# Clustered attention with two MLPs: the first head's first stacks written by copies, the third pair's norms two slots later, the first row of minima issued by ScalarE

## The chip, the cores and the metric

The kernel runs on one core of a Trainium2 chip. The metric is the device time of one execution in microseconds (us). The engines are named as in the profile: PE (TensorE, with PEld for its weight loads), DVE (VectorE), ACT (ScalarE), POOL (GpSimd) and SP (SyncE, which only issues transfers).

## The reference

The inputs are q, k and v (2 batches, 8 heads, 768 positions, 64 columns), 16 centroids a head, and the weights of two MLPs. Attention runs only between positions whose query and key have the same nearest centroid:

```python
q_n = q / (norm(q) + 1e-06)          # k_n, c_n in the same way
q_assign = argmax(einsum('bhsd,hcd->bhsc', q_n, c_n), axis=-1)
k_assign = argmax(einsum('bhsd,hcd->bhsc', k_n, c_n), axis=-1)
scores = q @ k.T / sqrt(64)
scores = where(q_assign[..., None] == k_assign[..., None, :], scores, -1e9)
scores = scores - max(scores, axis=-1)
attn = exp(scores); attn = attn / (sum(attn, axis=-1) + 1e-09)
x = (attn @ v), all heads side by side          # 1536 x 512
x = ((x @ w1) * (x @ w2)) @ w3 @ w_out          # first MLP
out = softplus(x @ w_in) @ w_out2               # second MLP
```

## The kernel before

**Pairs and slots.** The 16 heads are handled in 8 pairs; head hd is 2*pi + j. A head has 6 chunks of 128 queries, and the attention loop has one slot for each (96, and 10 more to drain). In slot s, `mx_pe` multiplies one chunk of queries with all keys into the PSUM bank mb (two matmuls, L600), and `mx_red` takes the extreme value of each row from it (L609, tile mn, a TENSOR_REDUCE on VectorE). There is one such bank, so the matmuls of a slot wait for the reduction of the slot before. Every 6 slots `m_row` turns a head's six columns of minima into a row (L616, L63, tile mr) and a DMA (L620) puts it into the head's q tile. Nine slots after its minima a chunk's scores are computed (`st_pe`, L630), exponentiated (`st_exp`, L637), and one slot later multiplied with v (`av_pe`, L645).

**Stacks.** The matmuls do masking and splitting in one go, by stacking rows: a head's tiles q and k have 128 rows and two parts, n = 0 and 1. Rows 0 to 63 hold the high part H of the transposed q or k, rows 64 to 95 a piece of the other operand's low part L, rows 96 and on the one-hot of the cluster (part 0), or the row of minima and a row of ones (part 1). The minima need part 0 alone. H and L come from a transpose (`t1_pe`, L307) and its evictions (`t1_ev`, L318 on ScalarE, L319 on VectorE); both hold q in rows 0 to 63 and k in rows 64 to 127, one tile for each head of a pair. `t_dma` moves them into the stacks by seven DMAs (L335 to L340), issued by SP, after a memset of the row of ones (L333, POOL). The one-hot rows go from PSUM to a tile sg (`back_ev`, L416) and from there by DMA (`m_dma`, L422).

**The clusters of a pair.** `load_qk` (L198) loads q and k of a pair into rawqk, of which there is one buffer. `norm_sq` squares it (L256 on POOL, or L258 on ScalarE), `norm_fold` adds pieces on POOL (L266, from the third pair on), `norm_sum` adds up on VectorE (L274), then come the root and reciprocal (L281 to L297). `sims_pe` and `simsT_pe` multiply with the centroids (L353, L373), `assign` finds the best cluster (L386 to L400), `back_pe` transposes the one-hots back (L410).

**The centroids** are normalised at the start on VectorE, in column operations (`centroid_prep`, L215 to L228).

**What sets the order.** Everything runs in the order in which it is written, under a manual schedule: each engine takes its instructions in that order and waits for what they need. The first pair is handled ahead of the slots. The second pair's steps are listed by slot in the tables PE1 and EV1, those of the later pairs in PE and EV, as an offset from the pair's first slot 2*QC*pi (QC is 6), so that the entry -18 of the third pair falls in slot 6. `steps` goes through these. Beside all this runs the preparation of the weight product (`w_step`, lines L63 and L465 to L474: load, scale, bits; w3r and w3d are its tiles). Its first two tiles are decoded between the first pair's one-hots and the first slot's minimum.

Of the kernel before, what the change touches and what calls it, by code (L numbers as in the profile page):

```python
# [9 lines left out]
F32R = mybir.dt.float32r  # L10
BF16 = mybir.dt.bfloat16
I32 = mybir.dt.int32
AF = mybir.ActivationFunctionType
# [5 lines left out]
P = 128  # L19
# [3 lines left out]
def f32(ap):  # L23
    return ap.bitcast(F32)
# [3 lines left out]
def fused_kernel(ctx: ExitStack, tc, q, k, v, centroids, w1, w2, w3, wo, w_in, w_o2, out):  # L28
# [6 lines left out]
    nc = tc.nc  # L35
    B, H, S, D = q.shape
# [153 lines left out]
    def load_qk(pi, js=range(2), dma=dma_in):  # L190
        if pi >= NPAIR:
            return
        b, h0 = divmod(2 * pi, H)
        if js[0] == 0:
            QK[pi] = ap1.tile([P, 2, QC, 2, D], F32, tag="rawqk", name=f"rawqk{pi}")
        for j in js:
            for ni, src in enumerate((q, k)):
                dma(  # L198
                    QK[pi][:, j, :, ni, :], src[b, h0 + j].rearrange("(p c) d -> p c d", p=P)
                )  # L200
# [51 lines left out]

    def norm_sq(pi, j):
        sq = ring.tile([P, QC, 2, D], F32, tag="w3k", name=f"sq{pi}_{j}")
        if pi >= 2:
            nc.gpsimd.tensor_tensor(out=sq, in0=QK[pi][:, j], in1=QK[pi][:, j], op=ALU.mult)  # L256
        else:
            nc.scalar.activation(sq, QK[pi][:, j], AF.Square)  # L258
        PR["sq", j] = sq
# [65 lines left out]
    def t_dma(pi, j):  # L325

        hd = 2 * pi + j
        a, l = f32(PR["H", j]), f32(PR["L", j])  # L330
        qt = QT[hd] = apT.tile([P, 2, S], F32R, tag="q", name=f"q{hd}")
        kt = KT[hd] = apT.tile([P, 2, S], F32R, tag="k", name=f"k{hd}")
        nc.gpsimd.memset(f32(kt[96:97, 1, :]), 1.0)  # L333
        dma = nc.sync.dma_start
        dma(f32(qt[:D]), a[:D].unsqueeze(1).to_broadcast([D, 2, S]))  # L335
        dma(f32(kt[:D, 0, :]), a[D:])
        dma(f32(kt[:D, 1, :]), l[D:])
        for n in range(2):
            dma(f32(qt[D : D + 32, n, :]), l[32 * n : 32 * n + 32])
            dma(f32(kt[D : D + 32, n, :]), a[D + 32 * n : D + 32 * n + 32])  # L340

    SG = ((0, 512), (512, S))

    def sims_pe(pi, g):
        if g == 0:
            PR["sT"] = ring.tile([P, S], F32, tag="w3k", name=f"sT{pi}")
        h0 = (2 * pi) % H
        m = take()
        c0, c1 = SG[g]
        n = 0  # L350
        for j in range(2):
            for t in (PR["H", j], PR["L", j]):
                nc.tensor.matmul(  # L353
                    m[:, : c1 - c0], cst[:, h0 + j, :], t[:, c0:c1],
                    start=(n == 0), stop=(n == 3),
                )
                n += 1
        PR["sm", g] = m
# [53 lines left out]

    def back_ev(pi):

        sg = PR["sg"] = ring.tile([P, S], F32R, tag="w3k", name=f"sg{pi}")
        nc.scalar.activation(sg, PR["bk"][:, :S], AF.Copy, scale=bigcol[:, 0:1])  # L416
        give(PR["bm"])
# [195 lines left out]
    def m_row(g):  # L613

        m = take()
        nc.tensor.transpose(m[:QC, :P], MN.pop(g), identF)  # L616
        t = sp.tile([QC, P], F32R, tag="mr", name=f"mr{g}")
        act_copy(t, m[:QC, :P], scale=-1.0)
        give(m)
        nc.sync.dma_start(f32(QT[g][96:97, 1, :]), f32(t))  # L620


    def st_pe(j):
# [200 lines left out]
    def pgo(o, f, *a):  # L824
        tc.cur_priority -= o
        f(*a)
        tc.cur_priority += o

    def steps(tab, s):
        for pi in range(2, NPAIR):  # L830
            for f, *a in tab.get(s - 2 * QC * pi, ()):
                if f is not load_qk or pi > 2:
                    f(pi, *a)


    PE1 = {
# [2 lines left out]
    }  # L839
    EV1 = {  # L840
        0: [(t1_ev, 0), (norm_sq, 0)], 1: [(t1_ev, 1), (norm_sum, 0)], 2: [(t1_ev, 2), (norm_sq, 1), (t_dma, 0)],
        3: [(t1_ev, 3), (norm_sum, 1), (norm_root,)], 4: [(sims_ev, 0), (norm_rec, 0), (norm_rec, 1), (t_dma, 1)],
        5: [(sims_ev, 1), (norm_rec, 2)], 7: [(assign, 0)], 8: [(assign, 1)],
        9: [(back_ev,)], 10: [(m_dma, 0), (m_dma, 1)],
    }

# [9 lines left out]
    with tc.manual_schedule():  # L856
        act_dma = nc.scalar.dma_start
        load_qk(0, [0])
        centroid_load()
        load_qk(0, [1], act_dma)  # L860
        nc.scalar.preload_act_table_set("natural_log_exp_and_others")
        w_load()
        w_load()
        t1_pe(0, 0)
        t1_pe(0, 1)
        centroid_prep()
        t1_ev(0, 0)
        t1_ev(0, 1)
        t1_pe(0, 2)
        t1_pe(0, 3)  # L870
        t1_ev(0, 2)
        t1_ev(0, 3)
        t_dma(0, 0)
        centroid_turn()
        norm_sq(0, 0)
        norm_sq(0, 1)
        sims_pe(0, 0)
        sims_pe(0, 1)
        sims_ev(0, 0)
        sims_ev(0, 1)  # L880
        norm_sum(0, 0)
        norm_sum(0, 1)
        simsT_pe(0)
        norm_root(0)
        norm_rec(0, 0)
        norm_rec(0, 1)
        norm_rec(0, 2)
        t_dma(0, 1)
        load_qk(1)
        assign(0, 0)  # L890
        assign(0, 1)
        back_pe(0)
        back_ev(0)
        m_dma(0, 0, act_dma)
        m_dma(0, 1, act_dma)
        w_load()
        load_v(0)
        while wk[0] < W0:
            w_next()
        for s in range(NSLOT + ML + AL):  # L900
            j = s - ML
            a = j - AL
            if s < NSLOT:
                mx_pe(s)
                mx_red(s)
            if s and s % QC == 0 and s <= NSLOT:
                m_row(s // QC - 1)
            weights = s >= ML
            if weights:
                w_step(wk[0], "hlpqe")  # L910
            if a > 0 and a % 3 == 0:
                av_ev(a // 3 - 1)
            for tab in (PE1, EV1):
                for f, *x in tab.get(s, ()):
                    f(1, *x)
            if s == 4:
                load_qk(2)
            if s == 6:
                load_v(1)
            steps(PE, s)  # L920
            steps(EV, s)
            if 0 <= j < NSLOT:
                st_pe(j)
                st_exp(j)
            if weights:
                w_step(wk[0], "Abcds")
            if 0 <= a:
                av_pe(a)
            if weights:
                w_step(wk[0], "Tm")  # L930
                wk[0] += 1

            for g in range(NH):
                r = s - (ML + AL + QC * g + QC - 1)
                if r in (2, 4, 6):
                    r_ev(g, r // 2 - 1)
                if r == 8:
                    x_norm(2 * g)
                    x_norm(2 * g + 1)
            if wk[0] == NWSTEP:  # L940
                feed.load(3)
            if s == NSLOT + 1:
                feed.take(2)
                taken += 2
# [176 lines left out]
```

## Time and profile before

| | |
|---|---|
| Time, median of 3 runs | 859.72 us (858.72 to 859.75) |
| Profiled execution | 858.86 us, span 857.1 us |
| Busy share of the span | PE 94%, DVE 58%, ACT 46%, POOL 28% |
| First matmuls of the minima (slot 0) | 28.00 us after the span's start |

The profile shows one execution; its span runs from the first instruction to the last, and the time of the execution is 1.76 us longer. The shares are means over the whole program; the attention loop and the MLPs behind it keep PE nearly full, its beginning does not.

### The profile page before, as it was taken

The page shows a single profiled execution, that of the slowest core. Times are in us where ns is not written, and L with a number is a line of the kernel's source. Part 1 is how long each engine was busy: PE and PEld are TensorE (multiplying, and loading weights), DVE is VectorE, ACT ScalarE, POOL GpSimd, SP SyncE. Part 2 cuts the span into 40 slices and gives each one's busy share as a digit, 9 for nine tenths or more (in the row PEclk, how much of TensorE's full clock was granted, in tenths as well). Part 3 has the DMA queues.
Part 4 walks back from the last instruction along what each step waited for, and adds up shares of the span by engine and source line. Part 5 has one row for each costly group of instructions (what it writes and reads, how often), then busy time and mean ns, then how long its engine had stood idle before and what let it go on. Part 6 is the DMA issues. An engine that isn't in the chain of part 4 may idle for free.

```text
span 857.1 us, 10095 instructions
## 1 busy us (share of the span) xinstructions
PE 801.5 (94%) x3553; PEld 636.8 (74%) x3553; DVE 492.9 (58%) x823; ACT 396.5 (46%) x683; POOL 242.7 (28%) x229
## 2 busy tenths in 40 slices
PE   4549999998999999989999999999999999999997
PEld 3337677776777777758888888887877788888886
DVE  5646766575676564438453254663988644454442
ACT  3315454454453444464443235454564644455443
POOL 2032333153414021135411113231344222222221
PEclk9969999999999999999999999999999999999999
DMA  7755756646545354026511114340120000001001
GB/s 195 186 106 136 182 133 137 162 115 171 154 111 119 85 157 104 21 68 185 169 49 50 50 50 147 99 148 0 50 74 1 25 26 1 1 0 50 1 1 50
DMA packets 77827, 76.40 MB, mean 89 GB/s; under 512 B 46416, under 2 KB 62928, under 8 KB 77776
## 3 DMA queue, kind: packets, MB, share of 16 engines
q1 hardware_dynamic: 76016, 74.96, 33.0%
q10 hardware_dynamic: 1760, 0.79, 0.4%
q8 instruction: 28, 0.46, 0.2%
q14 instruction: 23, 0.19, 0.1%
HBM read 50.41 MB, written 3.24 MB: 63 GB/s over the span
## 4 chain that ended last, share of the span: by engine, by line
PE 73%; DVE 12%; DMA 6%; issue 3%; ACT 2%; SPq 2%; POOL 1%; ACTq 0%; DVEq 0%; POOLq 0%
PE avb L645 10%; PE rb L793 8%; PE sb L793 8%; PE sb L1009 6%; PE mb L1052 6%; PE sb L630 6%; PE rb L1009 5%; PE rb L515 5%; PE mb L815 4%; PE mb L600 3%; PE rb L1052 3%; PE avb L1052 3%; PE avb L815 2%; PE rb L815 2%; DVE mn L609 2%
## 5 line engine op out<-in xcount | busy, mean ns | idle before, releaser
L609 DVE TENSOR_REDUCE mn<-mb 128x1 f32<-128x768 f32 x96 | 91.6, 954 | 92.5 <-PE mb L600 92.2
L645 PE MATMUL avb<-E,v 128*128 128x384 f32 x384 | 142.4, 493 | 0.4 <-ACT t L61 0.4
L66 POOL TENSOR_TENSOR u<-u,t 128x512 f32<-128x512 f32 x48 | 68.4, 1427 | 170.5 <-DVE u L1032 170.5
L637 ACT ACTIVATE E<-sb 128x768 f32<-128x768 f32 x96 | 77.7, 809 | 68.0 <-PE sb L630 67.0
L630 PE MATMUL sb<-q,k 128*128 128x384 f32 (+1 forms) x384 | 91.3, 360 | 7.6 <-ACT E L637 7.6
L645 PEld LDWEIGHTS avb<-E,v 128*128 128x128 f32 x384 | 71.9, 192 | 28.3 <-ACT t L61 1.8
L600 PE MATMUL mb<-k,q 128*128 128x384 f32 x192 | 69.8, 446 | 20.2 <-DVE mn L609 15.6
L630 PEld LDWEIGHTS sb<-q,k 128*128 128x128 f32 (+1 forms) x384 | 66.9, 193 | 14.1 <-ACT E L637 11.2
L1009 PE MATMUL sb<-ys,wh_i 128*128 128x512 f32 x192 | 64.1, 395 | 3.5 <-ACT t L1020 2.3
L600 PEld LDWEIGHTS mb<-k,q 128*128 128x128 f32 x192 | 36.0, 202 | 41.0 <-DVE mn L609 21.4
L1009 PE MATMUL rb<-ys,wh_i 128*128 128x512 f32 x192 | 63.4, 392 | 0.0
L793 PE MATMUL rb<-xs,wh 128*128 128x512 f32 x192 | 61.7, 392 | 0.0
L793 PE MATMUL sb<-xs,wh 128*128 128x512 f32 x192 | 61.7, 392 | 0.0
L1022 DVE TENSOR_SCALAR u<-t 128x512 f32<-128x512 f32 x48 | 21.4, 446 | 67.2 <-ACT t L1021 67.2
L66 POOL TENSOR_TENSOR wl_o<-d_o,wh_o 128x512 fp32r<-128x512 f32 x16 | 21.6, 1351 | 120.8 <-ACT wh_o L61 120.8
L69 DVE TENSOR_TENSOR gl<-u,gh 128x512 fp32r<-128x512 f32 x48 | 39.6, 824 | 19.5 <-ACT gh L61 19.0
L692 POOL TENSOR_TENSOR xT<-t,R 64x384 f32<-64x384 f32 x32 | 34.0, 1081 | 52.7 <-DMA R<-rd 52.6
L1031 ACT ACTIVATE u<-u 128x512 f32<-128x512 f32 x48 | 30.4, 633 | 35.9 <-DVE t L1028 35.6
L1009 PEld LDWEIGHTS sb<-ys,wh_i 128*128 128x128 f32 x192 | 35.9, 188 | 13.7 <-ACT t L1020 3.4
L318 ACT ACTIVATE H<-rb,qkcol 128x384 fp32r<-128x384 f32 x32 | 18.6, 582 | 53.5 <-PE rb L307 39.6
L1009 PEld LDWEIGHTS rb<-ys,wh_i 128*128 128x128 f32 x192 | 36.1, 188 | 8.1
L793 PEld LDWEIGHTS rb<-xs,wh 128*128 128x128 f32 x192 | 36.1, 188 | 7.9
(175 smaller groups left out, 1789.1 us busy)
## 6 DMA issues: line engine op xcount, KB each, us to landing
w3r<-in_moe_w_dram SPq DMA_DIRECT2D x16, 512.0 KB
w12r<-in_moe_w_dram SPq DMA_DIRECT2D x16, 512.0 KB
wir<-in_moe_w_in_dram SPq DMA_DIRECT2D x16, 512.0 KB
wor<-in_moe_w_out_dram SPq DMA_DIRECT2D x16, 512.0 KB
q<-H SPq DMA_DIRECT2D x16, 384.0 KB
w3r<-in_moe_w_out_dram SPq DMA_DIRECT2D x8, 512.0 KB
k<-H SPq DMA_DIRECT2D x16, 192.0 KB
k<-L SPq DMA_DIRECT2D x16, 192.0 KB
```

The costliest lines, as they stand in the source:

```text
L66: nc.gpsimd.tensor_tensor(out=o, in0=i, in1=hi, op=ALU.subtract)
L69: return nc.vector.tensor_tensor(out=o, in0=i, in1=hi, op=ALU.subtract)
L515: nc.tensor.matmul(m, a[:, ks], bb, start=(mc == 0 and x == 0), stop=(mc == NK - 1 and x == 2))
L600: nc.tensor.matmul(mbank[:, hf, :HALF], QT[g][:, 0, c * P : (c + 1) * P], KT[g][:, 0, hf * HALF : (hf + 1) * HALF], start=True, stop=True,)
L609: nc.vector.tensor_reduce(out=MN[g][:, c : c + 1], in_=mbank[:, :, :HALF], op=ALU.min, axis=AX.XY)
L630: nc.tensor.matmul(sbank[:, i, :HALF], KT[g][: P - 31 * n, n, ks], QT[g][: P - 31 * n, n, qs], start=(n == 0), stop=(n == 1),)
L637: nc.scalar.activation(E[j], sbank[:, :, :HALF], AF.Exp, scale=-1.0)
L645: nc.tensor.matmul(avbank[:, :HALF], V[g][:, 2 * kp + i, :], e[:, i, :], start=(kp == 0 and i == 0), stop=(kp == 2 and i == 1),)
L793: nc.tensor.matmul(bk[:, :BLK], a[:, sl], bb, start=(n == 0), stop=(n == 3 * CC - 1))
L815: nc.tensor.matmul(ybank[e][:, :BLK], a[:, es], bb, start=(fc == 0 and n == 0), stop=(fc == NFC - 1 and n == 2),)
L1009: nc.tensor.matmul(hbank[(bl * NF2 + fc) % 4][:, :BLK], a[:, sl], bb, start=(n == 0), stop=(n == 3 * CC - 1))
L1052: nc.tensor.matmul(ob, a[:, sl], bb, start=(fc == 0 and n == 0), stop=(fc == NF2 - 1 and n == 2),)
```

## The change

It has five parts.

- The squares of the first pair (`norm_sq`) run on POOL and no longer on ScalarE.
- The parts n = 0 of head 0's stacks are no longer made by transfers. `t_first` copies the H rows on ScalarE (64x768, twice), and the pieces of 32 rows on POOL; `back_ev` of the first pair writes the one-hot rows of head 0 from PSUM on ScalarE, ahead of sg, and the two transfers of `m_dma(0, 0)` are gone. `t_dma(0, 0)` keeps four transfers, for the parts n = 1, and is issued after `t_dma(0, 1)`; its loop now does n = 1 first, for all heads.
- `load_qk(1)` is issued ahead of all transfers of the first pair's stacks, and not after them.
- The norm steps of the third pair run two slots later; `t_dma(1, 1)` moves from slot 4 to slot 5, so that it is issued behind `load_qk(2)`; `load_v(1)` moves from slot 6 to slot 8.
- The DMA of head 0's row of minima is issued by ScalarE and not by SP.

PE keeps its order.

```diff
--- before.py
+++ after.py
@@ -252,7 +252,7 @@
 
     def norm_sq(pi, j):
         sq = ring.tile([P, QC, 2, D], F32, tag="w3k", name=f"sq{pi}_{j}")
-        if pi >= 2:
+        if pi != 1:
             nc.gpsimd.tensor_tensor(out=sq, in0=QK[pi][:, j], in1=QK[pi][:, j], op=ALU.mult)
         else:
             nc.scalar.activation(sq, QK[pi][:, j], AF.Square)
@@ -328,16 +328,34 @@
 
         hd = 2 * pi + j
         a, l = f32(PR["H", j]), f32(PR["L", j])
-        qt = QT[hd] = apT.tile([P, 2, S], F32R, tag="q", name=f"q{hd}")
-        kt = KT[hd] = apT.tile([P, 2, S], F32R, tag="k", name=f"k{hd}")
-        nc.gpsimd.memset(f32(kt[96:97, 1, :]), 1.0)
+        if hd:
+            t_tiles(hd)
+        qt, kt = QT[hd], KT[hd]
         dma = nc.sync.dma_start
-        dma(f32(qt[:D]), a[:D].unsqueeze(1).to_broadcast([D, 2, S]))
-        dma(f32(kt[:D, 0, :]), a[D:])
+        if hd:
+            dma(f32(qt[:D]), a[:D].unsqueeze(1).to_broadcast([D, 2, S]))
+            dma(f32(kt[:D, 0, :]), a[D:])
+        else:
+            dma(f32(qt[:D, 1, :]), a[:D])
         dma(f32(kt[:D, 1, :]), l[D:])
-        for n in range(2):
+        for n in range(2 if hd else 1):
+            n = 1 - n
             dma(f32(qt[D : D + 32, n, :]), l[32 * n : 32 * n + 32])
             dma(f32(kt[D : D + 32, n, :]), a[D + 32 * n : D + 32 * n + 32])
+
+    def t_tiles(hd):
+        QT[hd] = apT.tile([P, 2, S], F32R, tag="q", name=f"q{hd}")
+        KT[hd] = apT.tile([P, 2, S], F32R, tag="k", name=f"k{hd}")
+        nc.gpsimd.memset(f32(KT[hd][96:97, 1, :]), 1.0)
+
+    def t_first():
+
+        a, l = f32(PR["H", 0]), f32(PR["L", 0])
+        t_tiles(0)
+        act_copy(QT[0][:D, 0, :], a[:D])
+        act_copy(KT[0][:D, 0, :], a[D:])
+        nc.gpsimd.tensor_copy(KT[0][D : D + 32, 0, :], a[D : D + 32])
+        nc.gpsimd.tensor_copy(QT[0][D : D + 32, 0, :], l[:32])
 
     SG = ((0, 512), (512, S))
 
@@ -412,6 +430,12 @@
 
     def back_ev(pi):
 
+        if pi == 0:
+            for ni, d in enumerate((QT, KT)):
+                r = slice(64 * ni, 64 * ni + 32)
+                nc.scalar.activation(
+                    d[0][96:, 0, :], PR["bk"][r, :S], AF.Copy, scale=bigcol[r, 0:1]
+                )
         sg = PR["sg"] = ring.tile([P, S], F32R, tag="w3k", name=f"sg{pi}")
         nc.scalar.activation(sg, PR["bk"][:, :S], AF.Copy, scale=bigcol[:, 0:1])
         give(PR["bm"])
@@ -617,7 +641,7 @@
         t = sp.tile([QC, P], F32R, tag="mr", name=f"mr{g}")
         act_copy(t, m[:QC, :P], scale=-1.0)
         give(m)
-        nc.sync.dma_start(f32(QT[g][96:97, 1, :]), f32(t))
+        (nc.sync if g else nc.scalar).dma_start(f32(QT[g][96:97, 1, :]), f32(t))
 
 
     def st_pe(j):
@@ -826,11 +850,14 @@
         f(*a)
         tc.cur_priority += o
 
+    NORM = (norm_sq, norm_fold, norm_sum, norm_root, norm_rec)
+
     def steps(tab, s):
         for pi in range(2, NPAIR):
-            for f, *a in tab.get(s - 2 * QC * pi, ()):
-                if f is not load_qk or pi > 2:
-                    f(pi, *a)
+            for d in (0, 2):
+                for f, *a in tab.get(s - 2 * QC * pi - d, ()):
+                    if (d == 2) == (pi == 2 and f in NORM) and (f is not load_qk or pi > 2):
+                        f(pi, *a)
 
 
     PE1 = {
@@ -839,8 +866,8 @@
     }
     EV1 = {
         0: [(t1_ev, 0), (norm_sq, 0)], 1: [(t1_ev, 1), (norm_sum, 0)], 2: [(t1_ev, 2), (norm_sq, 1), (t_dma, 0)],
-        3: [(t1_ev, 3), (norm_sum, 1), (norm_root,)], 4: [(sims_ev, 0), (norm_rec, 0), (norm_rec, 1), (t_dma, 1)],
-        5: [(sims_ev, 1), (norm_rec, 2)], 7: [(assign, 0)], 8: [(assign, 1)],
+        3: [(t1_ev, 3), (norm_sum, 1), (norm_root,)], 4: [(sims_ev, 0), (norm_rec, 0), (norm_rec, 1)],
+        5: [(sims_ev, 1), (norm_rec, 2), (t_dma, 1)], 7: [(assign, 0)], 8: [(assign, 1)],
         9: [(back_ev,)], 10: [(m_dma, 0), (m_dma, 1)],
     }
 
@@ -870,10 +897,11 @@
         t1_pe(0, 3)
         t1_ev(0, 2)
         t1_ev(0, 3)
-        t_dma(0, 0)
         centroid_turn()
         norm_sq(0, 0)
         norm_sq(0, 1)
+        load_qk(1)
+        t_first()
         sims_pe(0, 0)
         sims_pe(0, 1)
         sims_ev(0, 0)
@@ -886,12 +914,11 @@
         norm_rec(0, 1)
         norm_rec(0, 2)
         t_dma(0, 1)
-        load_qk(1)
+        t_dma(0, 0)
         assign(0, 0)
         assign(0, 1)
         back_pe(0)
         back_ev(0)
-        m_dma(0, 0, act_dma)
         m_dma(0, 1, act_dma)
         w_load()
         load_v(0)
@@ -915,7 +942,7 @@
                     f(1, *x)
             if s == 4:
                 load_qk(2)
-            if s == 6:
+            if s == 8:
                 load_v(1)
             steps(PE, s)
             steps(EV, s)
```

On POOL, at the start, from the centroids' square root (L211) to the memsets of the stacks (k) and of v, before:

```order
L211 TENSOR_TENSOR cs<-cs,half_c 128x1
L333 MEMSET k_195 1x768
L290 TENSOR_TENSOR nrm_228<-nrm_228 128x24
L291 TENSOR_TENSOR nrm_228<-nrm_228 128x24
L333 MEMSET k_246 1x768
L569 MEMSET v_0_282 128x6x64
L569 MEMSET v_1_285 128x6x64
```

and after (L349 is the former L333, L357 and L358 are the copies of `t_first`, L593 the former L569):

```order
L211 TENSOR_TENSOR cs<-cs,half_c 128x1
L256 TENSOR_TENSOR sq_0_203<-rawqk_146 128x768
L256 TENSOR_TENSOR sq_1_205<-rawqk_146 128x768
L349 MEMSET k_213 1x768
L357 CAST k_213<-H_0_158 32x768
L358 CAST q_212<-L_0_159 32x768
L290 TENSOR_TENSOR nrm_230<-nrm_230 128x24
L291 TENSOR_TENSOR nrm_230<-nrm_230 128x24
L349 MEMSET k_248 1x768
L593 MEMSET v_0_283 128x6x64
L593 MEMSET v_1_286 128x6x64
```

The two squares of the first pair, one memset and two copies now stand directly behind L211, ahead of the norms' products (L290).

On ScalarE, from the second step of the first pair's root to the scaling of the first weight tiles (w3r), before (L422 are DMA issues):

```order
L283 ACTIVATE nrm_228<-nrm_228 128x24
L416 ACTIVATE sg_274<-rb_102,bigcol 128x768
L422 DMA q_194<-sg_274 32x768
L422 DMA k_195<-sg_274 32x768
L422 DMA q_245<-sg_274 32x768
L422 DMA k_246<-sg_274 32x768
L63 ACTIVATE w3r_154<-w3r_154 128x512
L63 ACTIVATE w3r_156<-w3r_156 128x512
```

and after (L436 are the added one-hot rows, L440 the former L416, L446 the former L422):

```order
L283 ACTIVATE nrm_230<-nrm_230 128x24
L436 ACTIVATE q_212<-rb_102,bigcol 32x768
L436 ACTIVATE k_213<-rb_102,bigcol 32x768
L440 ACTIVATE sg_277<-rb_102,bigcol 128x768
L446 DMA q_247<-sg_277 32x768
L446 DMA k_248<-sg_277 32x768
L63 ACTIVATE w3r_154<-w3r_154 128x512
L63 ACTIVATE w3r_156<-w3r_156 128x512
```

Two ACTIVATEs stand ahead of sg, and two DMA issues of four are gone ahead of the scaling L63.

On VectorE, around the minima (mn) of slots 6 to 9, before (L274 of nrm_418 is the third pair's sum, L386 to L400 are the second pair's `assign`):

```order
L609 TENSOR_REDUCE mn_398<-mb 128x1
L274 TENSOR_REDUCE nrm_418<-sq_0_382 128x12
L609 TENSOR_REDUCE mn_398<-mb 128x1
L386 TENSOR_TENSOR rb_101<-rb_101,nrm_319 128x384
L387 TENSOR_REDUCE mx_423<-rb_101 128x24
L388 TENSOR_TENSOR rb_101<-rb_101,mx_423 128x384
L609 TENSOR_REDUCE mn_398<-mb 128x1
L394 TENSOR_TENSOR rb_101<-rb_101,wfirst 128x384
L395 TENSOR_REDUCE mx_423<-rb_101 128x24
L400 TENSOR_TENSOR oh<-rb_101,mx_423 128x6x2x16 x2
L319 SCALAR_TENSOR_TENSOR L_0_437<-rb_102,qkcol,H_0_436 128x384
L609 TENSOR_REDUCE mn_398<-mb 128x1
```

and after (L633 is the former L609, L404 to L418 the former L386 to L400):

```order
L633 TENSOR_REDUCE mn_395<-mb 128x1 x2
L404 TENSOR_TENSOR rb_101<-rb_101,nrm_320 128x384
L405 TENSOR_REDUCE mx_412<-rb_101 128x24
L406 TENSOR_TENSOR rb_101<-rb_101,mx_412 128x384
L633 TENSOR_REDUCE mn_395<-mb 128x1
L412 TENSOR_TENSOR rb_101<-rb_101,wfirst 128x384
L413 TENSOR_REDUCE mx_412<-rb_101 128x24
L418 TENSOR_TENSOR oh<-rb_101,mx_412 128x6x2x16 x2
L319 SCALAR_TENSOR_TENSOR L_0_432<-rb_102,qkcol,H_0_431 128x384
L274 TENSOR_REDUCE nrm_440<-sq_0_407 128x12
L633 TENSOR_REDUCE mn_395<-mb 128x1
```

The sum stood between the minima of slots 6 and 7; now it stands between those of slots 8 and 9, behind the assignment and an L319.

## Rows read from the trace of the kernel before

**Rows 1.** Stretches: length, busy us of PE, PEld, DVE, ACT, POOL; PEclk, DMA share, GB/s.

```profile
0.00:28.00 28.00, 9.86 (x40) 7.82 (x40) 13.60 (x57) 8.14 (x15) 6.30 (x16) 1.00 0.66 162
28.00:46.40 18.40, 13.30 (x49) 9.83 (x49) 13.62 (x21) 6.18 (x13) 1.21 (x3) 1.00 1.03 239
46.40:56.06 9.66, 0.03 (x2) 0.01 (x1) 1.28 (x3) 0.00 (x0) 4.34 (x6) 0.70 0.85 153
56.06:70.30 14.24, 11.49 (x46) 8.71 (x47) 11.23 (x21) 6.87 (x12) 3.16 (x6) 0.72 0.28 66
70.30:857.10 786.80, 766.78 (x3419) 610.40 (x3419) 453.17 (x722) 375.27 (x644) 227.70 (x200) 0.99 0.30 83
```

**Rows 2.** Timeline of PE: start, us, line, [idle before <- releaser].

```profile
28.00 0.98 PE L600 MATMUL mb<-k,q 128*128 128x384 f32 x2 [4.06 <-DMA k<-sg]
...
32.26 0.99 PE L600 MATMUL mb<-k,q 128*128 128x384 f32 x2
...
45.83 0.59 PE L600 MATMUL mb<-k,q 128*128 128x384 f32 x2
56.06 1.01 PE L600 MATMUL mb<-k,q 128*128 128x384 f32 x2 [9.63 <-DVE mn L609]
```

**Rows 3.** Waits, 20 to 75 us: total, times, longest.

```profile
DVE nrm L274 <- POOL sq L266: 9.2, 1, 9.2
```

**Rows 4.** Chain that ended last: start us, us, what.

```profile
9.82 0.92 PE rb L307 x3
...
23.98 0.91 ACT sg L416
...
27.82 3.78 DMA rawqk<-in_k_dram
...
51.56 1.48 POOL sq L256
...
65.38 4.84 DMA k<-sg
```

**Rows 5.** Timeline of ACT, 6 to 32 us.

```profile
11.24 1.56 ACT L258 ACTIVATE sq<-rawqk 128x768 f32<-128x768 f32 x2
...
27.50 1.24 ACT L63 ACTIVATE w3r<-w3r 128x512 f32<-128x512 f32 x2 [2.62 <-DMA k<-sg]
```

**Rows 6.** Timeline of DVE, 27 to 64 us.

```profile
30.66 0.95 DVE L609 TENSOR_REDUCE mn<-mb 128x1 f32<-128x768 f32 x1
...
60.17 0.61 DVE L319 SCALAR_TENSOR_TENSOR L<-rb,qkcol,H 128x384 fp32r<-128x384 f32 x1
```

**Rows 7.** Timeline of SP's DMA issues around t_dma(1,1).

```profile
40.26 0.67 SPq L335 DMA_DIRECT2D q<-H  x1
...
45.87 0.62 SPq L198 DMA_DIRECT2D rawqk<-in_q_dram  x1
```

**Rows 8.** Timeline of POOL, 7 to 17 us.

```profile
7.74 0.73 POOL L333 MEMSET k<- 1x768 f32 x1
```

**Rows 9.** Timeline of DVE, 7 to 11 us.

```profile
8.18 0.22 DVE L217 SCALAR_TENSOR_TENSOR cs<-cs 128x1 f32<-128x1 f32 x1
...
8.82 0.42 DVE L228 TENSOR_SCALAR cn<-cw,cs 128x64 f32<-128x64 f32 x2
```

**Rows 10.** Timeline of DVE at two other places.

```profile
18.15 0.80 DVE L293 TENSOR_SCALAR nrm<-nrm 128x24 f32<-128x24 f32 x1 [0.73 <-POOL nrm L291]
...
337.75 1.52 DVE L670 TENSOR_SCALAR r<-r 128x6 f32<-128x6 f32 x1 [0.88 <-DMA r<-sd]
```

**Rows 11.** Timeline of POOL at the same two places.

```profile
18.17 0.73 POOL L333 MEMSET k<- 1x768 f32 x1
...
336.56 1.97 POOL L692 TENSOR_TENSOR xT<-t,R 64x384 f32<-64x384 f32 x2 [10.95 <-DMA R<-rd]
338.47 0.78 POOL L569 MEMSET v<- 128x384 f32 x2
```

**Rows 12.** Line L670: duration ns min/median/max, first and last start us.

```profile
L670 DVE TENSOR_SCALAR r<-r x16: 108/161/1524, 94.9 to 398.3; 128x6 f32<-128x6 f32 x16
```

## The prediction

> **What bounds the kernel now.** I read the busy time of each engine by stretches first [rows 1]. From 70.3 us to the end TensorE is busy 766.78 of 786.80 us; the change touches nothing there but a few load orders, so I count that stretch as it is. What can move lies in the first 70 us, where TensorE is busy 9.86 of 28.00, 13.30 of 18.40, 0.03 of 9.66 and 11.49 of 14.24 us. The third of these is a hole of nearly ten microseconds in which ScalarE does nothing and VectorE 1.28 us.
>
> The matmul pairs of the minima (L600) give the pace there [rows 2]: slot 0 starts at 28.00, slot 1 at 32.26, slot 7 at 45.83, slot 8 at 56.06, after 9.63 us of waiting for a minimum; slot 12 is where the last stretch begins, at 70.30. The waits name what stood behind that [rows 3]: VectorE's sum of squares of the third pair (L274) waited 9.2 us for GpSimd's fold. VectorE works in order, so the minimum of slot 7 stood behind that sum, and with it TensorE.
>
> The chain of what ended last shows how the first slots come about [rows 4]. It runs through VectorE's column work on the centroids and L319 behind it, the transpose that waited for L319 (9.82), and much later the one-hot rows (sg, 23.98, 0.91) and their transfers. The matmuls of slot 0 need the last of those transfers, so they start only at 28.00. The next piece of this chain is the load of rawqk for the second pair, which lands at 27.82 + 3.78 = 31.60: slot 1 stands behind transposes that need it. The square of the third pair begins only at 51.56, when its load has landed too.
>
> **The change, part by part.** The sum is made against the profiled execution (858.86 us); the median of the three runs is 859.72, 0.86 above it, and I add that at the end.
>
> *Copies in place of the transfers of the one-hots.* ScalarE now writes the two rows of head 0 itself, before sg. Both are ACTIVATEs over 768 columns like sg, 0.91 each, so slot 0 may start at 23.98 + 2 x 0.91 + 0.05 = 25.85 in place of 28.00, 2.15 earlier. But the first minimum doesn't follow: it stands on VectorE behind the decoding of two weight tiles, which begins with ScalarE's scaling L63, at 27.50 now [rows 5]. ScalarE's own order is what that hangs on. Before: sg and four DMA issues; after: three ACTIVATEs (2.73) and two issues (four take from 24.89 to 27.50 now, so 1.3). So L63 starts at 23.98 + 2.73 + 1.3 = 28.0, half a microsecond later, and the first minimum at 30.66 [rows 6] + 0.5 = 31.2. It ends at 32.15, and slot 1 starts at 32.17 where it was 32.26, if rawqk is there by then, and it is: load_qk(1) is now ahead of all stack transfers on SP's queue. **Gain 0.1**, not 2.15. The two large copies (64 x 768) replace ScalarE's two squares of as many elements a row (1.56 for both) [rows 5] in the same place of its queue: no cost.
>
> *The stall.* The sum L274 of the third pair now stands behind the minima of slots 7 and 8, the second pair's assignment and an L319, and rawqk of that pair is issued ahead of t_dma(1,1)'s seven transfers. With nothing between them, slot 7's minimum follows its matmuls as the others do: 45.83 + 0.59 + 0.05 = 46.47, ends at 47.42, and slot 8 starts at 47.47 in place of 56.06. **Gain 8.6.** What is late next: that L319 ends at 60.17 + 0.61 = 60.78 now [rows 6], 4.7 after slot 8's start; so VectorE reaches the sum at 47.47 + 4.7 = 52.2. The seven transfers of t_dma(1,1) took SP from 40.26 to 45.87 [rows 7]; the load goes out 5.6 earlier, lands at about 51.56 - 5.6 = 46.0, and the first square and its folds, 51.56 to 54.78 now, end at 49.2. That is 3 us of slack; without the earlier landing 2.6 us of the stall come back (a rival).
>
> *Slots 8 to 12.* They took 14.24 us, in part at a lower clock (mean 0.72 [rows 1]), because the hole let the granted clock fall. Without the hole they may run faster (at most 0.9, since VectorE is busy 11.23 of the 14.24), or the one-hots of head 2 hold slot 12: their issue on SP stands behind a weight load that waits for VectorE's L474, and the landing alone takes 4.84 [rows 4], which doesn't shrink (0.45 more at most). I take **0**. ScalarE's queue for the first row of minima costs 0.7 of ScalarE's issue time where it has little else; it takes the issue from behind the loads of rawqk on SP, and st_pe of slot 9 is the first to need it. No cost.
>
> *Squares and copies on GpSimd.* These cost, I think. Before, GpSimd did one memset of 0.73 at 7.74 beside VectorE's column work [rows 8, 9]. After, it has two squares of 128x768 (1.48 each [rows 4]), then the memset, then a copy of H (32x768), all back to back from 7.70. VectorE runs at that time L217 (two inputs in SBUF, at 8.18) and L228 (TENSOR_SCALAR on 128x64, at 8.82). Does a VectorE instruction wait for GpSimd? Twice the trace shows it [rows 10 to 12]: L293 takes 0.80 on 24 elements beside a memset of 0.73, and both end within 0.05 of each other; L670 (also a TENSOR_SCALAR), 0.16 at the median, starts at 337.75 and ends at 339.27, when the second of two multiplications (336.56 to 338.53) and two memsets behind it (to 339.25) are over. It didn't get in between them. So:
> - Low end: L217 gets in between the squares (first one 7.70 to 9.18), its followers run to 9.8, L228 waits for the second square (which gave 0.23 to L217): 9.18 + 0.23 + 1.48 = 10.9 in place of 8.82: 2.1, with the gap 2.2.
> - Upper end: L228 is held as L670 was, through the memset (10.9 + 0.73 = 11.6) and the copy of H, whose price no row has: between a memset of as many elements a row (0.73) and a square (1.48), 12.3 to 13.1. That is 3.5 to 4.3 later. The second copy needs L and so stands behind VectorE again.
>
> L228 is the same operation as L670, so I take the upper way, with the copy at the memset's price: **cost 3.5**, with 2.2 and 4.3 for the range. Below 2.2 lies only the case that nothing is held (a rival). All of it is on the path: L319 stands right behind L228, the transpose at 9.82 waited for L319, and the chain leads on from it to the one-hots.
>
> The Trainium skill speaks of this lock: "SBUF — State Buffer", section "Who interferes with whom", says that GpSimd and VectorE share one pair of ports as an exclusive lock, that an instruction with two SBUF inputs contends with a GpSimd instruction that reads SBUF and not with one that only writes, and that a tensor_scalar in the 2-port mode contends. The trace agrees on L217 beside the memset (0.22, not held) and L293 beside it (0.80, held). [...]
>
> *Sum.* -0.1 - 8.6 + 0 + 3.5 = -5.2: 853.7 by the profiled execution, **854.5** beside the median.
>
> **The rivals.**
> - *Nothing is held on GpSimd.* For it: L217 is short, and L670 takes 0.16 at the median [rows 12]. Against it: the two held ones [rows 10]. Then the cost is 0 and the time 854.5 - 3.5 = 851.0. Chance 0.15.
> - *The lower clock through slots 8 to 12.* TensorE's work there is 11.49 x 0.72 = 8.3 us at the full level, 16.5 at half. If these slots run wholly at the lower of the two levels (1.2 GHz), they take 16.5 to 17 in place of 14.24, 2.3 to 3 more: 857.1. For it: TensorE is lightly loaded before, busy 13.30 of 18.40 from 28.00 to 46.40, and slots 0, 1 and 8 run at 0.98 to 1.01 a pair, where slot 7 at the high level takes 0.59 [rows 2]. Against it: the fall came within the hole, and the hole goes. Chance 0.18.
> - *A new wait behind the old.* Either the third pair's load lands no earlier, and 2.6 of the stall return, or head 2's one-hot transfers take half as long again or twice as long as 4.84 (the DMA share was 0.28 when they ran, 0.85 to 1.03 in the stretches before [rows 1]), and slot 12 waits 2.4 to 4.8 longer: 856.9 to 859.3. Chance 0.11.
> - *The stall stays, and the time is slower.* If the third pair's load, whose issue on SP now stands directly behind t_dma(1,0), is held there or slowed by the stack transfers that follow it, the square starts too late and the sum holds VectorE in its new place. All of the gain of 8.6 is lost if the folds end at 52.2 + 8.6 = 60.8, with the load landing at 57.6; the cost on GpSimd remains: 859.72 - 0.1 + 3.5 = 863.1. The kernel is slower than before when more than 5.2 of the stall comes back, that is from a landing at 52.2 + 5.2 - 3.2 = 54.2 on. Against it: now the landing is at 51.56. Chance 0.06.
> - The forecast itself, 852.3 to 855.8 by the two ends of the GpSimd cost and 0.9 for the slots: chance 0.50.
>
> **How the numbers follow.** 0.2% of this time is 1.7 us, about what a measurement can tell from no change, so 858.0 and 861.4 are the bounds. The forecast, the first two rivals and half of the new wait lie below 858.0 (faster 0.86); the rest of the new wait and small parts of the clock's give same 0.08; the stall slower 0.06. The range 850.5 to 857.6 goes down to the case without holding and up to the clock's, and leaves out the stall, half of the new wait and a margin at both ends.
>
> **What would show it.** In the changed profile: no wait of the sum L274 for GpSimd of over 1 us; slot 8 within 2 us of slot 7; the squares at 7.70 and L228 that ends between 10.9 and 13.5, or at 9.2 if nothing is held; all that follows it (the last one-hot copy, slot 0) late by the same amount, less 2.15 for slot 0; L63 0.5 further behind the start of the one-hots' evictions; slots 8 to 12 in 13.3 to 14.7 with pairs of 0.6 if the clock stays high. It would be wrong above all if L228 is held for longer than the copy of H, if the clock falls, or if slot 12 waits for its one-hots.

## The result

The changed kernel takes 852.54 us (median of 9 runs, 850.61 to 856.68) where the kernel before takes 860.49 beside it (9 runs, 858.72 to 862.72). The ratio is 0.9912, with a 95% interval from 0.9889 to 0.9935: 7.6 us less, between 5.6 and 9.5. The prediction was 854.5, 5.2 less.

Its first profiled execution took 856.68, the longest of the nine; a second profile, of an execution of 852.39, lies close to the median. Both are shown here, the second first (it is that of the run e10_after_again, below). In the second the pairs of the minima on TensorE (L624, formerly L600) stand so; columns as in [rows 2]:

```profile
27.80 0.98 PE L624 MATMUL mb<-k,q 128*128 128x384 f32 x2 [1.98 <-ACT k L436]
...
34.09 1.01 PE L624 MATMUL mb<-k,q 128*128 128x384 f32 x2 [4.67 <-DVE mn L633]
...
47.18 0.60 PE L624 MATMUL mb<-k,q 128*128 128x384 f32 x2
48.83 0.62 PE L624 MATMUL mb<-k,q 128*128 128x384 f32 x2 [1.05 <-DVE mn L633]
...
63.39 0.58 PE L624 MATMUL mb<-k,q 128*128 128x384 f32 x2 [1.73 <-DMA k<-sg]
```

Slot 0 is 0.2 earlier than before, slot 1 is 1.8 later (34.09 for 32.26), slot 7 1.35 later (47.18 for 45.83), slot 8 7.2 earlier (48.83 for 56.06) and slot 12 6.9 earlier (63.39 for 70.30). The hole of [rows 1, 2] is gone: from slot 7 to slot 8 it is 1.65 where it was 10.23. The first profile shows the same places:

```profile
34.36 1.01 PE L624 MATMUL mb<-k,q 128*128 128x384 f32 x2 [4.67 <-DVE mn L633]
...
49.46 0.99 PE L624 MATMUL mb<-k,q 128*128 128x384 f32 x2
51.50 1.01 PE L624 MATMUL mb<-k,q 128*128 128x384 f32 x2 [1.05 <-DVE mn L633]
...
54.02 1.01 PE L624 MATMUL mb<-k,q 128*128 128x384 f32 x2 [0.88 <-DVE mn L633]
...
65.18 0.59 PE L624 MATMUL mb<-k,q 128*128 128x384 f32 x2
```

Here slots 7, 8 and 9 still run at 0.99 to 1.01, and slot 8 follows slot 7 at 2.04. In the second profile slots 7 and 8 take 0.60 and 0.62. By these durations the first execution came to the higher of TensorE's two levels later. Slot 8 starts 2.7 later than in the second profile, 0.3 of which is there at slot 1 already, and slot 12 starts 1.8 later; the other 2.5 of the difference between the two spans (854.9 and 850.6) arise after slot 12.

The wait of the third pair's sum for GpSimd's fold [rows 3] is in neither list of waits. What the second list has at these slots (total, times, longest):

```profile
PE mb L624 <- DVE mn L633: 10.2, 8, 4.7
...
PE mb L624 <- DMA k<-sg: 1.7, 1, 1.7
...
POOL sq L256 <- DMA rawqk<-in_k_dram: 1.2, 1, 1.2
```

TensorE's longest wait for a minimum is 4.7, and that lies between slots 0 and 1. Slot 12 waits 1.7 for head 2's one-hots.

The start pays. VectorE's column work on the centroids and GpSimd's queue in the second profile, to hold against [rows 8, 9]:

```profile
8.30 0.95 DVE L217 SCALAR_TENSOR_TENSOR cs<-cs 128x1 f32<-128x1 f32 x1
9.29 0.15 DVE L221 TENSOR_SCALAR cs<-cs 128x1 f32<-128x1 f32 x1
...
9.67 1.83 DVE L228 TENSOR_SCALAR cn<-cw,cs 128x64 f32<-128x64 f32 x2
10.79 1.65 DVE L319 SCALAR_TENSOR_TENSOR L<-rb,qkcol,H 128x384 fp32r<-128x384 f32 x3
```

```profile
7.24 0.56 POOL L211 TENSOR_TENSOR cs<-cs,half_c 128x1 f32<-128x1 f32 x1 [4.40 <-ACT csq L210]
7.76 2.90 POOL L256 TENSOR_TENSOR sq<-rawqk 128x768 f32<-128x768 f32 x2
10.72 0.73 POOL L349 MEMSET k<- 1x768 f32 x1
11.51 0.82 POOL L357 CAST k<-H 32x768 fp32r<-32x768 f32 x1
```

L217 takes 0.95 and ends with the first square, at 9.25; it took 0.22. The two L228 take 1.83 together, 1.04 and 0.87 each; the first gets through when the second square ends, at 10.66, and the second ends with the memset, at 11.45. They took 0.42. The copy of H (L357), which I had counted, starts only then. GpSimd's root (L211) is 0.13 later than before, so what is lost here is 11.5 - 9.24 less 0.13, about 2.1 on VectorE. Not all of it reaches TensorE: the first L319 starts at 10.79, while the second L228 is still held. The transpose that waits for L319 starts 1.8 later than the 9.82 of [rows 4]:

```profile
11.59 0.90 PE L307 MATMUL rb<-identF,rawqk 128*128 128x128 f32 x3 [2.59 <-DVE L L319]
```

And the first minimum stands where the prediction had it, behind the weight decoding, which stands behind ScalarE:

```profile
25.86 0.89 ACT L436 ACTIVATE q<-rb,bigcol 32x768 fp32r<-32x768 bf16 x1 [6.88 <-PE rb L428]
...
27.68 0.90 ACT L440 ACTIVATE sg<-rb,bigcol 128x768 fp32r<-128x768 bf16 x1
...
29.93 1.23 ACT L63 ACTIVATE w3r<-w3r 128x512 f32<-128x512 f32 x2 [1.35 <-issue]
```

```profile
30.62 0.69 DVE L493 SCALAR_TENSOR_TENSOR w3r<-w3r 128x512 int32<-128x512 int32 x1 [5.40 <-ACT w3r L63]
...
33.09 0.95 DVE L633 TENSOR_REDUCE mn<-mb 128x1 f32<-128x768 f32 x1
```

The matmuls of slot 0 end at 28.8; their minimum starts at 33.09, after L63 at 29.93 and the rest of the decoding.

### The profile page after: what moved, and what is told of

It is laid out like the page before. It is cut to its first block, busy times and chain, and to the rows that moved or that the text cites. A ratio compares the mean times of both kernels' runs of the same rounds, so it can differ in the third digit from the quotient of the medians.

```text
span 854.9 us, 10088 instructions
## 1 busy us (share of the span) xinstructions
PE 805.2 (94%) x3553; PEld 640.4 (75%) x3553; DVE 494.8 (58%) x823; ACT 398.0 (47%) x685; POOL 247.5 (29%) x233
## 4 chain that ended last, share of the span: by engine, by line
PE 76%; DVE 13%; issue 4%; ACT 3%; DMA 2%; SPq 1%; POOL 1%; ACTq 0%; DVEq 0%; POOLq 0%
PE avb L669 11%; PE rb L817 8%; PE sb L817 8%; PE sb L654 6%; PE sb L1036 6%; PE mb L1079 6%; PE rb L1036 5%; PE rb L539 5%; PE mb L839 4%; PE mb L624 4%; PE rb L1079 3%; PE avb L1079 3%; PE avb L839 2%; PE rb L839 2%; DVE mn L633 2%
## 5 line engine op out<-in xcount | busy, mean ns | idle before, releaser
L633 DVE TENSOR_REDUCE mn<-mb 128x1 f32<-128x768 f32 x96 | 91.6, 954 | 96.8 <-PE mb L624 96.5
L624 PE MATMUL mb<-k,q 128*128 128x384 f32 x192 | 71.2, 454 | 13.5 <-DVE mn L633 11.2
L624 PEld LDWEIGHTS mb<-k,q 128*128 128x128 f32 x192 | 36.6, 205 | 34.7 <-DVE mn L633 17.2
L817 PEld LDWEIGHTS sb<-xs,wh 128*128 128x128 f32 x192 | 36.1, 188 | 7.8
```

The lines of the kernel that those rows point to most:

```text
L624: nc.tensor.matmul(mbank[:, hf, :HALF], QT[g][:, 0, c * P : (c + 1) * P], KT[g][:, 0, hf * HALF : (hf + 1) * HALF], start=True, stop=True,)
L633: nc.vector.tensor_reduce(out=MN[g][:, c : c + 1], in_=mbank[:, :, :HALF], op=ALU.min, axis=AX.XY)
L817: nc.tensor.matmul(bk[:, :BLK], a[:, sl], bb, start=(n == 0), stop=(n == 3 * CC - 1))
```

## The experiments

Theory A is the prediction's: the hole was the third pair's sum in front of a minimum, the earlier load lets it stay away, GpSimd's squares hold VectorE, and the copies give nothing because the first minimum stands behind the decoding. Theory B: the gain comes from the start. Times are against runs of the kernel before on the same chip (medians 860.93 to 860.95), and differences are the ratio's, on 860.9.

**The squares back on ScalarE** (e1_sq_act):

```diff
-        if pi != 1:
+        if pi >= 2:
             nc.gpsimd.tensor_tensor(out=sq, ...
```

> The changed kernel with the first pair's squares back on ScalarE, all else as changed. Theory A (GpSimd's squares hold VectorE's column work): L217 takes 0.22 again, not 0.94, the two L228 together 0.4 to 1.2 (a copy of H stands beside them now), the transpose behind L319 starts 1.3 to 2.0 earlier than the 11.86 of the changed kernel's trace, and so does slot 0 (28.08); the time is 1.3 to 2 below that of the changed kernel, so 8.9 to 9.6 below before. Rival (the lateness came with the centroids' load, which landed 0.4 later in that execution, and the rest is made up later): L217 short or not, the time stays 7.6 below before.

Measured: 851.79, ratio 0.9897 (0.9881 to 0.9914), 8.9 less than before. Line L217 and line L228, then the pairs of slots 0 and 1 (for a line: duration in ns, min/median/max, first and last start):

```profile
L217 DVE SCALAR_TENSOR_TENSOR cs<-cs x1: 220/220/220, 8.1 to 8.1; 128x1 f32<-128x1 f32 x1
```

```profile
L228 DVE TENSOR_SCALAR cn<-cw,cs x2: 242/500/759, 8.8 to 9.4; 128x64 f32<-128x64 f32 x2
```

```profile
26.50 0.98 PE L624 MATMUL mb<-k,q 128*128 128x384 f32 x2 [1.98 <-ACT k L436]
...
32.79 1.01 PE L624 MATMUL mb<-k,q 128*128 128x384 f32 x2 [4.68 <-DVE mn L633]
```

L217 is back at 0.22, though GpSimd's memset runs beside it, one L228 at 0.24, and one at 0.76 beside the copy of H. Slot 0 starts 1.3 earlier than in the second profile and slot 1 too. So the squares hold VectorE, as the theory says. In the total, 0.7 less than the changed kernel by the medians, the intervals overlap; the time alone wouldn't show it.

**The norm steps alone** (e2_norms): the kernel before with the new `steps`, and nothing else of the change.

```diff
-            for f, *a in tab.get(s - 2 * QC * pi, ()):
-                if f is not load_qk or pi > 2:
-                    f(pi, *a)
+            for d in (0, 2):
+                for f, *a in tab.get(s - 2 * QC * pi - d, ()):
+                    if (d == 2) == (pi == 2 and f in NORM) and (f is not load_qk or pi > 2):
+                        f(pi, *a)
```

> The kernel before with the third pair's norm steps two slots later and nothing else. Theory A (the hole is the sum L274 in front of a minimum): slot 8 follows slot 7 at 2 us, the sum waits 2 to 3 us in its new place because the load still lands late, and the time is 5 to 6.5 below before. Theory B (the gain comes from the start, and the hole only moves): the sum waits over 6 us in its new place, and the time is at most 2 below before.

Measured: 853.69, ratio 0.9920 (0.9896 to 0.9943), 6.9 less, 0.4 more than theory A's range and far from B's. Theory A in the size, then, but the wait that is left isn't the one I expected. TensorE after slot 7:

```profile
47.30 0.62 PE L600 MATMUL mb<-k,q 128*128 128x384 f32 x2 [1.05 <-DVE mn L609]
52.87 0.90 PE L307 MATMUL rb<-identF,rawqk 128*128 128x128 f32 x3 [4.96 <-DMA rawqk<-in_k_dram]
53.42 0.99 PE L600 MATMUL mb<-k,q 128*128 128x384 f32 x2
```

Slot 8 follows slot 7 at 1.64. Then slot 9 comes 6.1 later: the third pair's transposes (L307) stand ahead of it on TensorE and wait for the same load, 4.96 us. The sum itself waits 1.1. So the late load has a second way to hold the slots, which the prediction didn't name.

**Norm steps and load order** (e3_norms_load): e2 with

```diff
-        4: [..., (norm_rec, 0), (norm_rec, 1), (t_dma, 1)],
-        5: [(sims_ev, 1), (norm_rec, 2)], ...
+        4: [..., (norm_rec, 0), (norm_rec, 1)],
+        5: [(sims_ev, 1), (norm_rec, 2), (t_dma, 1)], ...
-            if s == 6:
+            if s == 8:
                 load_v(1)
```

> As the run with the norm steps alone, and t_dma(1,1) one slot later, behind the third pair's load, and load_v(1) two slots later. Theory A: the third pair's rawqk lands some 5 us earlier, the sum waits under 0.5 us, and the time is 8 to 9 below before, more than the changed kernel's 7.6, since the start pays nothing to GpSimd. Rival (the landing is set by the traffic, not by the order of issue): the sum waits 2 to 3 us as in the run with the norms alone, and the time is that run's.

Measured: 851.07, ratio 0.9895 (0.9866 to 0.9923), 9.0 less. GpSimd's first square of the third pair here and in e2, and the pairs of slots 8 and 9:

```profile
46.59 1.47 POOL L256 TENSOR_TENSOR sq<-rawqk 128x768 f32<-128x768 f32 x1 [2.75 <-DMA rawqk<-in_k_dram]
```

```profile
52.90 1.47 POOL L256 TENSOR_TENSOR sq<-rawqk 128x768 f32<-128x768 f32 x1 [8.61 <-DMA rawqk<-in_q_dram]
```

```profile
47.33 0.62 PE L600 MATMUL mb<-k,q 128*128 128x384 f32 x2 [1.05 <-DVE mn L609]
...
49.84 0.62 PE L600 MATMUL mb<-k,q 128*128 128x384 f32 x2 [1.57 <-DVE mn L609]
```

The load lands 6.3 earlier: SP issues its first transfer at 40.53 where it was 46.57 in e2, and the transfers of v go out behind it in both. Slot 9 follows slot 8 at 2.5. The order of issue sets the landing. These two parts alone give as much as the whole change.

**The start alone** (e4_start_only): the changed kernel with the old `steps`, tables and load_v.

> The changed kernel without its norm move and without the two load moves that belong to it: copies, squares on GpSimd, load_qk(1) first, and the row of minima on ScalarE remain. Theory A: the hole of 9 us before slot 8 is there as before, slot 1 starts 1.5 to 2 later than 32.26, and the time is 1 to 2.5 above before. Theory B: the time is 4 or more below before.

Measured: 863.56, ratio 1.0032 (1.0015 to 1.0049), 2.8 more than before. The sum's wait and the pair of slot 8:

```profile
DVE nrm L274 <- POOL sq L266: 10.6, 1, 10.6
```

```profile
59.43 1.01 PE L624 MATMUL mb<-k,q 128*128 128x384 f32 x2 [11.09 <-DVE mn L633]
```

The hole is there, with 10.6, and slot 8 is 3.4 later than in [rows 2]. Theory B falls: the start costs. It costs a little more than expected, partly since the third pair's load goes out 4.3 later here (50.20 for the 45.87 of [rows 7]) and its first square starts 3.4 later, at 54.94, after GpSimd has waited 9.4 for it: as much as slot 8 is late.

**The squares on GpSimd alone** (e7_sq_pool): the kernel before with `pi != 1` in norm_sq.

> The kernel before with the first pair's squares on GpSimd and nothing else. Theory A (squares hold VectorE's column work by their reads): L217 0.9, L228 held to the end of the second square or of the memset behind it, slot 0 1.6 to 2.1 later than 28.00, and the time 1.5 to 2.5 above before. Rival (the lateness is taken up by the wait of slot 1 for the second pair's load): slot 1 within 0.5 of 32.26, and no change in time.

Measured: 861.92, ratio 1.0019 (1.0000 to 1.0037), 1.6 more, at the edge of what can be told from no change. The trace is clear:

```profile
7.92 0.73 POOL L333 MEMSET k<- 1x768 f32 x1
8.73 2.89 POOL L256 TENSOR_TENSOR sq<-rawqk 128x768 f32<-128x768 f32 x2
```

```profile
8.37 0.22 DVE L217 SCALAR_TENSOR_TENSOR cs<-cs 128x1 f32<-128x1 f32 x1
...
9.01 2.66 DVE L228 TENSOR_SCALAR cn<-cw,cs 128x64 f32<-128x64 f32 x2
```

```profile
30.43 0.98 PE L600 MATMUL mb<-k,q 128*128 128x384 f32 x2 [4.13 <-DMA k<-sg]
...
34.84 0.99 PE L600 MATMUL mb<-k,q 128*128 128x384 f32 x2
```

Here the memset stands ahead of the squares, and L217 beside it takes 0.22; I had expected 0.9. The two L228 take 2.66 (1.24 and 1.50), each held to the end of one square. Slot 0 is 2.4 later than in [rows 2], slot 1 2.6. The rival, that slot 1's wait takes it up, falls.

**The scaling ahead** (e5_early_scale): e1, with the scaling of the first two weight tiles (L63) ahead of the assignment on ScalarE.

```diff
+        for i in range(W0):
+            w_step(i, "A")
         assign(0, 0)
...
         while wk[0] < W0:
-            w_next()
+            w_next(WALL[1:])
```

> The changed kernel with the first pair's squares on ScalarE, and with the scaling of the first two weight tiles (L63) issued on ScalarE ahead of the first pair's assignment and not behind the one-hots. Theory A (the first minimum stood behind the weight decoding, which stood behind ScalarE's copies, so the copies could give nothing): the first minimum follows slot 0 at once, slot 1 starts at about 28.5 where it was 32.79 in the run with the squares on ScalarE, and the time is 3.5 to 4.5 below that run's, so 12.5 to 13.5 below before. Rival (the later slots wait for the second and third pair's loads and stacks, which set the pace anyway): slot 1 early, slot 8 or 12 late, and the time within 1 of that run's 9.1 below before.

Measured: 848.49, ratio 0.9853 (0.9831 to 0.9875), 12.7 less: with the two kernels built on it, the fastest measured. The pairs of slots 0, 1 and 12:

```profile
26.65 0.98 PE L624 MATMUL mb<-k,q 128*128 128x384 f32 x2 [1.98 <-ACT k L436]
...
28.68 1.01 PE L624 MATMUL mb<-k,q 128*128 128x384 f32 x2 [0.41 <-DVE mn L633]
...
59.37 0.58 PE L624 MATMUL mb<-k,q 128*128 128x384 f32 x2 [0.92 <-DMA k<-sg]
```

Slot 1 now follows slot 0 at 2.0, 4.1 earlier than in e1, and 3.3 of that is in the time by the medians (3.8 by the ratios). Slot 12 is 3.6 earlier than in e1: here the third pair's transposes wait 1.7 for their load ahead of slot 9. The scaling behind the one-hots was what kept the copies from giving anything.

**The scaling ahead, without the copies** (e6_scale_transfers): e3 with the same edit.

> The run with norms and loads moved in the kernel before, with the same early scaling; head 0's stacks by transfers, load_qk(1) behind all stack transfers. Theory A: slot 0 stays at 28.1, and slot 1 at 32, since the second pair's rawqk lands at 31.6 and its transposes stand ahead of slot 1 on TensorE: the time is within 0.5 of the 9 to 9.9 below before of the run without the early scaling. Rival (the decoding alone was the brake): slot 1 at about 30 and 2 to 3 faster than that run.

Measured: 852.34, ratio 0.9896 (0.9869 to 0.9924), 9.0 less, as e3. TensorE from slot 0 to slot 1:

```profile
28.28 0.98 PE L600 MATMUL mb<-k,q 128*128 128x384 f32 x2 [4.06 <-DMA k<-sg]
32.24 0.88 PE L307 MATMUL rb<-identF,rawqk 128*128 128x128 f32 x3 [2.98 <-DMA rawqk<-in_k_dram]
```

The transposes ahead of slot 1 wait for the second pair's load until 32.24. So the early scaling gives nothing without the start's other parts, and these give nothing without it (e1 beside e3). Whether it needs the copies, or the early load_qk(1) alone, isn't shown: these two were always run together.

**Nine matmuls to warm TensorE** (e8_warm): e5 with

```diff
+        for _ in range(9):
+            nc.tensor.matmul(sbank[:, 0, :], cst[:, 0, :], <cst of four heads>, start=True, stop=True)
         back_pe(0)
```

> The run with the early scaling, and nine matmuls of 128x512 on constant data into the unused scores bank, between the first pair's cluster matmuls and its back transposes, where TensorE idles; the output doesn't use them. Theory C (TensorE's lower level costs 0.4 in each of the first slots): the pairs of slots 0 to 5 take 0.6 and not 1.0, and the time is 1.5 to 2.5 below that run's. Rival (the level falls again before slot 1, or the nine don't raise it): the pairs take 1.0 up to slot 5 and the time is that run's.

Measured: 848.17, ratio 0.9847 (0.9823 to 0.9870), not to be told from e5.

```profile
26.28 0.76 PE L624 MATMUL mb<-k,q 128*128 128x384 f32 x2 [1.98 <-ACT k L436]
...
28.09 1.01 PE L624 MATMUL mb<-k,q 128*128 128x384 f32 x2 [0.41 <-DVE mn L633]
...
60.44 0.78 PE L624 MATMUL mb<-k,q 128*128 128x384 f32 x2 [3.48 <-DMA k<-sg]
```

Slot 0 takes 0.76, slot 1 1.01 again, and so do slots 2 to 4: the rival holds. Slot 12 waits 3.48 for head 2's one-hots in this profile.

**The second pair's one-hots ahead of the weight load** (e9_onehots_ahead): e5 with

```diff
-        9: [(back_ev,)], 10: [(m_dma, 0), (m_dma, 1)],
+        9: [(back_ev,), (m_dma, 0), (m_dma, 1)],
```

> The run with the early scaling, and the second pair's one-hot transfers (m_dma of pair 1) listed a slot earlier, so that SP issues them ahead of the weight load that waits for VectorE's decoding. Theory D (slot 12 waits for the landing of head 2's one-hots, 0.9 in that run's profile and 3.5 in that of the run with the nine matmuls): the issue follows sg's eviction within 1 us, slot 12 doesn't wait for k<-sg, and the time is 0.5 to 2.5 below that of the run with the early scaling (848.5). Rival (the landing of the third pair's load holds slot 9, and what slot 12 gains is lost in the next weight load): no change, 848 to 849.

Measured: 848.94, ratio 0.9853 (0.9830 to 0.9876), no change against e5: the rival's number, though its reason, the next weight load, isn't shown. The one-hots are issued 1.4 after sg's eviction ends (51.59 for 50.23), behind the loads of v, where it was 2.9 in e5. Slot 12 starts at 58.17 and waits 0.31. So the new order shortens that wait in the trace, but the time doesn't show it beyond the runs' spread (845.44 to 850.85).

**The changed kernel again** (e10_after_again):

> The changed kernel itself, for a second profile. If the 856.68 of the first profiled execution was 4 above the median of its runs because TensorE stayed at the lower level until 57 us there and because of single later waits (1.1 at 215 us, 1.3 to 3 around 380 us, 0.7 at 660 us), the second trace has those places at other sizes, and the first 70 us gain 5 to 7 on before in both; if the change itself costs at these later places, both traces show the same losses there. Time 7 to 8.5 below before.

Measured: 852.46 (851.04 to 853.37), ratio 0.9902 (0.9883 to 0.9921), 8.4 less. Its rows stand above. Both profiles have the same places at the start: L217 and the two L228 held, the first minimum behind the decoding, no hole. Up to slot 12 the gain on before is 6.9 here and 5.1 there, as expected. They differ in when TensorE's pairs get short (slot 7 at 0.60 here, slot 9 still at 1.01 there), and by 2.5 us after slot 12. That the change itself costs at later places isn't shown.

## Why the prediction came out as it did

**The sign and the mechanism were right**: the hole was the whole gain. Of its 8.6, the second profile shows 10.23 - 1.65 = 8.58, and e2 and e4 show that it comes with the norm steps and not with the start.

**The step that was mis-sized is the cost on GpSimd**, 3.5 in the sum and 1.8 on the path. L228 was to be held "as L670 was", through the memset and the copy, as if it were one instruction. It is two, and each was over with the one GpSimd instruction under way: the first with the second square, the second with the memset (1.04 and 0.87; in e7, with a square each, 1.24 and 1.50). So the pair ends at 11.50, about where the working has the end of the memset (11.6), and the copy of H, which brought it to 12.3, held nothing: 0.8 less. The working also set this end against the pair's former start, 8.82, where its former end was 9.24: 0.4 less. And the first L319 starts beside the second L228, so that the transpose stands 0.1 behind the pair's end (11.59) where it stood 0.6 behind it (9.82): 0.5 less. That leaves 1.8, below even the low end of 2.2.

I chose the branch by one row, L670 in [rows 10], because it was the same operation. The trace before has the other case too. Of VectorE and of GpSimd:

```profile
190.89 0.56 DVE L670 TENSOR_SCALAR r<-r 128x6 f32<-128x6 f32 x1
```

```profile
189.30 2.12 POOL L266 TENSOR_TENSOR sq<-sq 128x384 f32<-128x384 f32 x2
191.38 1.27 POOL L66 TENSOR_TENSOR wol<-w3d,woh 128x512 fp32r<-128x512 f32 x1
```

Here L670 ends at 191.45 with the fold under way (191.42), although the next product stands right behind it. And at the place of [rows 10] L670 is held through both memsets in before and in seven other runs, but in e3 and e4 it takes 0.81 and 0.75 and ends with the product. One row was no rule.

With 1.8 the sum is -6.9, 852.8 beside the median of before's first three runs; measured were 852.5. That the two lie so close is in part luck: the later medians of before are 0.8 to 1.2 higher, and the measured difference is 7.6 to 8.4.

**The held instructions.** That L217 with two SBUF inputs is held by a square and not by a memset, as the Trainium skill says ("SBUF — State Buffer", "Who interferes with whom"), is what the runs show: 0.95 beside a square, 0.22 beside a memset in e1 and e7. The rival that nothing is held falls with it. L221, a TENSOR_SCALAR like L228 but on a single element a row, was not held: it took 0.15 at 9.29 in the second profile, while the second square ran.

**The copies** were given 0.1 and not 2.15, and e1 beside e3 bears that out: slot 0 at 26.50, but slot 1 at 32.79, and 851.79 beside 851.07. In the second profile L63 starts 4.07 after the first one-hot copy (29.93 and 25.86), where it started 3.52 after sg [rows 4, 5]: the half microsecond of the working. e5 shows the reason, the scaling on ScalarE.

**The load's 5.6** were 5.05 in the second profile, in which the first square starts at 46.51 where it was 51.56, and 6.3 between e2 and e3. The slack was there: the folds end at 49.7 and the sum starts at 53.5. What it guards was told incompletely: besides the sum, TensorE's transposes of the third pair wait for it (e2).

**Slots 8 to 12** were to keep their 14.24. They took 14.56 in the second profile and 13.68 in the first. In the second, slot 12 waited 1.7 for its one-hots; the stretch as a whole is 0.32 longer, within the 0.45.

**The lower clock through slots 8 to 12** is answered both ways. In the second profile slots 7 and 8 run at 0.60 and 0.62. In the first slots 8 and 9 run at 1.01, and slots 8 to 12 took 13.68 all the same: that rival's 2.3 to 3 more were not there. What the lower level cost in the first lies earlier, 17.1 from slot 1 to slot 8 against 14.7.

What stays open: why L670 was held through three GpSimd instructions in some runs, and through one in others, as each L228 was; by what the single executions spread by up to 6 us; and what the first row of minima on ScalarE and the early load_qk(1) do by themselves, as neither was run alone.

## What to carry to other kernels

Before pricing a faster step, look at what its consumer's engine does next: the copies made slot 0 ready 4 us before its minimum could start, and only moving the decoding's first step gave that time back. When work is moved to GpSimd, list what VectorE runs beside it: those of its instructions that were held at the start took up to 1.5 us each, and of the 2.3 by which VectorE was later 1.8 reached TensorE. Before one row is taken for a rule, look for every other case of it in the trace: here the second case, which would have warned of the choice, stood in the profile before. A wait that is moved away by order should be followed to each engine that reads the same load, not only to the one that was named in the list of waits.

## What the runs showed of the hardware

The granted clock and the durations don't always tell the same. Of the same stretch, before the rise, in the second and in the first profile (columns as in [rows 1]):

```profile
28.00:40.00 12.00, 5.92 (x19) 4.34 (x20) 7.80 (x12) 4.91 (x8) 0.00 (x0) 0.50 0.50 120
```

```profile
28.00:40.00 12.00, 5.85 (x18) 4.30 (x19) 7.63 (x11) 5.16 (x8) 0.00 (x0) 1.00 0.56 135
```

The granted clock is 0.50 in one and 1.00 in the other, while the pairs of slot 1 take 1.01 in both. In the second profile slots 7 and 8, at 0.60 and 0.62, lie in a stretch granted 1.00, so the pair's duration tells the two levels apart there; that the first profile lacks a fall ahead of its first entry is likely, but isn't shown. [rows 1] reads 1.00 from the start up to 46.40 as well, with pairs of 0.98 and 0.99 in slots 0 and 1 [rows 2].
